# A fused attention, FFN and gated-convolution kernel: a new table of planner ranks and step durations, and eight instead of four ReLU buffers

## The chip, the cores and the metric

The kernel runs on one core of one Trainium2 chip. The metric is the device time of one execution in microseconds (us). The engines are named as in the profile: PE (TensorE matmul), PEld (its weight loads), DVE (VectorE), ACT (ScalarE), POOL (GpSimd) and SP (SyncE, which issues the DMAs here).

## What is computed

Three layers follow each other on 4 sequences of 576 positions with 512 features (18 tiles of 128 rows).

```python
q_rot, k_rot = rotate(q), rotate(k)               # 8 heads of 64
scores = (q_rot @ k_rot.T) / sqrt(64)
attn = exp(scores - max(scores)); attn /= attn.sum() + 1e-9
x = attn @ v                                      # heads side by side: 512 features
xn = (x - mean) / sqrt(var + 1e-6) * g_ln
x = x + relu(xn @ w_ch1) @ w_ch2                  # 512 -> 2048 -> 512, float64 weights
gate = sigmoid(causal depthwise convolution of x, 5 taps)
out = (gate * (x @ w_val)) @ w_out
```

## The kernel before, in words

**Attention.** The 576x576 score matrix of every head is cut into 144 tiles of 128 query rows. One tile passes through scores on PE (`a_scores`: L499 with float32 operands in batch 0, L504 with split float32r operands afterwards), the negated row maximum on DVE (`a_max`, L509), the exponential on ACT (`a_exp`, L515), its float16 part on ACT (`a_hi`, L521) and the rest of it on DVE (`a_lo`, L526), a transposing DMA issued by SP (`a_turn`, L531), and the product with V on PE (`a_pv`, L550 and L553). Before that q and k are rotated on DVE (`mul`, L314 and L316; `add`, L324; `lo`, L344), and V is scaled and split by ACT and DVE (L415, L441, L446, L450, L451); its scale comes from a maximum on DVE (`vmax0`, L424 and L137 to L139, for the four first ones together).

**Weights.** The FFN's float64 weights are loaded as 16 pieces of 1 MB (L649), put together by ACT and DVE (L658, L655, L662), bounded by matmuls on PE (`products`, L678, 128 of them), and split into two float16 halves (L716 on ACT, L719 on DVE).

**FFN.** For each of the 18 row tiles: LayerNorm on DVE, POOL and ACT (L786 to L809), a transposing DMA (L814), and then four times a step `f1` on PE (48 matmuls, L824), `relu` on ACT (L836, which writes `hh`), `hlo` on DVE (L842, which writes `hl`), and `f2` on PE (12 matmuls, L852). `ffn_out` on DVE adds the result (L856). `hh` and `hl` live in `FH` pairs of buffers; the four pairs of row tile 0 lie elsewhere.

**Gate and projection.** The last layer works on nine pairs of row tiles: a turn through `rope_sb` (DVE copy L948, DMA, DVE copy L960), two float32r halves (L968 on ACT, L973 on DVE), and then for four blocks of features the gate (ACT L979, four or eight taps on DVE in `gate_b`, L988, ACT sigmoid L992), the values (`val`, 12 matmuls on PE, L1001), their product (DVE L1006) and its halves (`val_b` ACT L1012, `val_c` DVE L1016, in one buffer `gv`), and at last `proj` on PE (L1028, twice 12 matmuls).

**What sets the order.** No hardware scheduler chooses. While the program is built, `plan.step` records every step with an engine, a duration that the author states, a rank and its dependencies; `Plan.run` replays them against those durations, and whenever an engine is free it takes, among the steps that are ready within `NEAR` us, the one of the lowest rank. SP's transfers have `RATE`, `T_LAG` and `AHEAD`. Ranks are a constant per kind of step (`R_SC`, `R_F1`, `R_GATE`, ...) plus a running number, and `..._LEAD` puts loads and rotations ahead of the tile that needs them. What comes out is one fixed list of instructions per engine, and every engine works through its own list in that order, waiting on semaphores. The constants stand at the head of the file.

Of the kernel before, what the change touches and what calls it, by code (L numbers as in the profile page):

```python
# [23 lines left out]
XN_SCALE = 2.0  # L24
W1_SCALE = 2.0 ** 10
W2_SCALE = 2.0 ** 15
PT, P16, FH = 4, 3, 4
QS, K_LEAD = 3, 6
T_LAG, RATE, NEAR, AHEAD = 2.4, 280.0, 0.15, 2.0
XT, KQ, RAW, GT, X3, GV = 3, 2, 3, 6, 2, 1  # L30

QK_LEAD_0, QK_LEAD, V_LEAD_0, V_LEAD, LD_LEAD, W_LEAD = 30, 8, 28, 6, 4, 6
R_W1, S_W1, R_W2, S_W2 = 3, 1, 16, 2
R_GAIN, R_TINY, R_LN, R_RELU, R_FO, R_OUT = 0, -900, -300, -200, -250, -20
R_SC, R_PV, R_F1, R_F2 = 0, -4, 1000, 900
# [17 lines left out]
class Plan:  # L53
# [3 lines left out]
    RATE, NEAR, AHEAD = RATE, NEAR, AHEAD  # L57
# [98 lines left out]
def kernel(ctx: ExitStack, tc: tile.TileContext, qk, v, g_ln, w_ch1, w_ch2, w_val, conv_w, w_out, rope, eye, out):  # L156
# [20 lines left out]
    plan = Plan(dict(raw0=RAW, raw=RAW, qx=2, qs=QS, kf0=1, kf1=1, kf2=1, kf3=1, qf=QS, k20=1, k21=1, k22=1, k23=1, kx0=1, kx1=1, kx2=1, kx3=1, kq=KQ, qd=1, qdf=1, vt0=NP, sv0=1, vt=1, vh=NP, sv=4, vb=2, vm=2, ss=2, so=1, nmx=4, p32=2, p16=P16, pT=PT,  # L177
                     hp=2, acc=1, wr0=3, wr1=2, ln=1, xn=1, x16=1, xT=XT, fh=FH, r3=4, t3=4, xT3=2, tx=1, x3=X3, gt=GT, gv=GV, pv=3, po=2))
# [3 lines left out]
    DVE, ACT, PE, SP, POOL = "DVE", "ACT", "PE", "SP", "POOL"  # L182
# [353 lines left out]
    def a_pv(i):  # L536
        p, h, c0 = tiles[i]
        pT = live.pop(i)
        vh, vl = prep_v(p)["vh"], prep_v(p)["vl"]
        g, j = group_of[i]  # L540
        if j == 0:
            ovs[g] = ps_o.tile([128, 6, D + 1], F32, name="ov", tag="ov")
        ov = ovs[g]
        if h is None:
            o, hs, nh = ov[:, 0:2], 0, 2
        else:
            j += tiles[groups[g][0]][1] is None
            o, hs, nh = ov[:, j:j + 1], h, 1
        for c in range(9):
            nc.tensor.matmul(o, pT[:, c], vh[:, 2 * c + hs:2 * c + hs + nh], start=(c == 0), stop=(c == 8))  # L550

            if c < 5:
                nc.tensor.matmul(o[..., 0:D], pT[:, c], vl[:, 2 * c + hs:2 * c + hs + nh], start=False, stop=False)  # L553
# [42 lines left out]
    for i in range(NS):  # L596
        p, h, c0 = tiles[i]
        b = parts[p][0]
        bf, vf = bufs[p], bufs[base[p]]
        if h != 1:  # L600
            ne = 1 if h is None else 2
            ss = [Buf("ss") for _ in range(ne)]
            x = plan.step(PE, (1.6 if h is None else 2.2) if b == 0 else 0.9 if h is None else 1.05, R_SC + i, lambda i=i: a_scores(i), after=bf["ready"] + ([bf["dg"]] if h is None else []), takes=ss,
                          uses=([bf["qd"]] if h is None else []) + [vf["kq"], bf["q"]], row="sc")
            attention.append(x)
            if p < NP:
                early.append(x)
            if b == 1:
                kx_users.append(x)
            for e in range(ne):  # L610
                j = i + e
                nm, p32, p16, pT = Buf("nmx"), Buf("p32"), Buf("p16"), Buf("pT")
                y = plan.step(DVE, dve(S), R_MX + j, lambda j=j: a_max(j), after=[x], takes=[nm], uses=[ss[e]])
                y = plan.step(ACT, act(S), R_EXP + j, lambda j=j: a_exp(j), after=[y], takes=[p32], uses=[nm, ss[e]], row="exp")
                y = plan.step(ACT, act(S), R_EXP + j, lambda j=j: a_hi(j), after=[y], takes=[p16], uses=[p32])
                y = plan.step(DVE, dve(S), R_LO + j, lambda j=j: a_lo(j), after=[y], uses=[p32, p16])
                y = plan.step(SP, 1.0, R_TURN + j, lambda j=j: a_turn(j), after=[y], takes=[pT], uses=[p16], size=TURN, row="turn")
                tile_done[j] = (y, pT)
    for g, ts in enumerate(groups):
        so = Buf("so")  # L620
        p = tiles[ts[0]][0]
        vf = bufs[base[p]]
        last = None
        for k, i in enumerate(ts):
            y, pT = tile_done[i]
            last = plan.step(PE, 0.82 if tiles[i][1] is None else 0.42, R_PV + i, lambda i=i: a_pv(i), after=[y, last] + vf["v"], takes=[so] if k == 0 else [], uses=[pT, vf["vh"]] + ([so] if k else []), row="pv")
        b, pr, n, lead, m = out_of(g)
        x = plan.step(DVE, 0.24 + m * 0.14 + (0.1 if m else 0), R_OUT + ts[-1], lambda g=g: a_rd(g), after=[last], uses=[so, vf["sv"]])
        o = [x]
        if lead:  # L630
            o.append(plan.step(ACT, 0.32, R_OUT + ts[-1], lambda g=g: a_lead(g), after=[x], uses=[so]))
        outs[g] = o
        attention.extend(o)
# [235 lines left out]
    for n in range(NT):  # L869
        ln, xn, x16, xT, acc = Buf("ln"), Buf("xn"), Buf("x16"), Buf("xT"), Buf("acc")  # L870
        x = plan.step(DVE, 1.0, R_LN + n, lambda n=n: ln_a(n), after=rows[n] + [e_ffn], takes=[ln], row="ln")
        x = plan.step(POOL, 1.3, R_LN + n, lambda n=n: ln_p(n), after=[x], uses=[ln])
        x = plan.step(DVE, 0.47, R_LN + n, lambda n=n: ln_b(n), after=[x], takes=[xn], uses=[ln])
        x = plan.step(ACT, act(512), R_LN + n, lambda n=n: ln_c(n), after=[x], takes=[x16], uses=[xn])
        x = plan.step(DVE, dve(512), R_LN + n, lambda n=n: ln_d(n), after=[x], uses=[xn, x16])
        x = plan.step(SP, 1.0, R_LN + n - 100, lambda n=n: ln_t(n), after=[x], takes=[xT], uses=[x16], size=TURN)
        f2s = None
        prev = None
        for f in range(0, KF, FE):
            k = n * 4 + f // FE  # L880
            hp, fh = Buf("hp"), Buf("fh")
            prev = plan.step(PE, 2.7, R_F1 + k, lambda n=n, f=f: f1(n, f), after=[x, w_ready[0, f // 2 + 1], prev], takes=[hp] + ([fh] if n else []), uses=[xT], row="f1")
            y = plan.step(ACT, act(512), R_RELU + k, lambda n=n, f=f: relu(n, f), after=[prev], uses=[hp] + ([fh] if n else []), row="relu")
            y = plan.step(DVE, dve(512), R_RELU + k, lambda n=n, f=f: hlo(n, f), after=[y], uses=[hp] + ([fh] if n else []))
            f2s = plan.step(PE, 2.6, R_F2 + k, lambda n=n, f=f: f2(n, f), after=[y, w_ready[1, f // 2 + 1], f2s], takes=[acc] if f == 0 else [], uses=([acc] if f else []) + ([fh] if n else []), row="f2")
            if n == 0:
                pend_hid[5 + f // FE] = f2s
        done.append(plan.step(DVE, dve(512), R_FO + n, lambda n=n: ffn_out(n), after=[f2s], uses=[acc]))
# [245 lines left out]
```

## Time and profile before

| what | value |
|---|---|
| time, median of 3 runs | 742.03 us (741.21 to 745.29) |
| profiled execution | 743.6 us, of which the span from first to last instruction is 741.8 us |
| mean granted TensorE clock | 0.961 of full speed |
| busy PE, PEld, DVE, ACT, POOL | 681.0, 531.2, 631.1, 459.3, 16.9 us |
| DMA | 103.62 MB, 66.3% of 16 engines over the span |

A busy time is the time in which the engine had an instruction in work, and the ends of matmuls are modelled, so a PE that is shown busy may hold a matmul that waits. "Granted clock" is the share of the full TensorE clock. A window row gives busy time and number of instructions for every engine in one stretch of the span.

### The profile page before, as it was taken

The numbers are of one execution on the slowest core, as the hardware profiler recorded it, in microseconds if no ns is written. First come the engines' busy times: TensorE is split into PE (matmuls) and PEld (weight loads), VectorE is DVE, ScalarE is ACT, GpSimd is POOL, SyncE is SP. The second block draws the span as 40 slices with busy tenths as digits, with TensorE's granted clock in tenths as the row PEclk, the third lists the DMA queues.
The fourth block names the chain that finished last, engine by engine and source line by source line (L and its number), as shares of the span: only waits on it lengthen the run. The fifth ranks groups of instructions, "written<-read, shape, count | busy, mean of one in ns | idle before, by whom it ended". The sixth has DMA issues, their size and how long they took to land.

```text
span 741.8 us, 19303 instructions
## 1 busy us (share of the span) xinstructions
PE 681.0 (92%) x7929; PEld 531.2 (72%) x7929; DVE 631.1 (85%) x1365; ACT 459.3 (62%) x802; POOL 16.9 (2%) x40
## 2 busy tenths in 40 slices
PE   3446879899999999999999999999999989999998
PEld 1334768557777787778777877787777867787886
DVE  6999989999898999989998988987566999877664
ACT  5888976869666577757567876665282443344332
POOL 0000000000000000000000000000000000000000
PEclk9965878999999999999999999999999998999999
DMA  8999997578887997779869778865574132221011
GB/s 307 259 296 271 281 218 158 93 179 132 153 133 139 163 163 150 132 133 166 156 133 193 140 109 134 137 111 97 110 206 73 29 86 58 58 57 44 30 43 57
DMA packets 239288, 103.62 MB, mean 140 GB/s; under 512 B 211168, under 2 KB 227552, under 8 KB 239200
## 3 DMA queue, kind: packets, MB, share of 16 engines
q1 hardware_dynamic: 239200, 102.39, 66.3%
q8 instruction: 62, 1.02, 0.6%
q14 instruction: 26, 0.21, 0.1%
HBM read 45.73 MB, written 4.72 MB: 68 GB/s over the span
## 4 chain that ended last, share of the span: by engine, by line
PE 56%; DVE 28%; ACT 7%; DMA 5%; issue 3%; SPq 0%; ACTq 0%; DVEq 0%
PE hp L824 16%; PE acc L852 16%; PE po L1028 6%; PE sc L504 5%; DVE gt L988 4%; PE pv L1001 4%; PE ov L550 4%; DVE p L526 4%; DVE nmx L509 3%; DMA pT<-p 3%; DVE raw L316 2%; PE ov L553 2%; ACT p L521 2%; ACT p L515 2%; DVE hl L842 2%
## 5 line engine op out<-in xcount | busy, mean ns | idle before, releaser
L824 PE MATMUL hp<-xT,wall 128*128 128x128 f16 x3456 | 206.3, 220 | 0.0
L824 PEld LDWEIGHTS <-wall 128*128 128x128 f16 x3456 | 196.8, 98 | 6.7 <-issue 2.0
L852 PE MATMUL acc<-wall,hh 128*128 128x512 f16 x544 | 163.8, 383 | 2.1 <-DVE gt L988 2.1
L515 ACT ACTIVATE p<-sc,nmx 128x576 f32<-128x576 f32 x144 | 105.8, 736 | 68.0 <-DVE nmx L509 66.8
L526 DVE SCALAR_TENSOR_TENSOR p<-p,p 128x576 f16<-128x576 f32 x144 | 108.1, 753 | 21.4 <-ACT p L521 21.0
L509 DVE TENSOR_REDUCE nmx<-sc 128x1 f32<-128x576 f32 x144 | 106.1, 749 | 1.6 <-PE sc L504 0.9
L852 PE MATMUL acc<-wall,hl 128*128 128x512 f16 x272 | 104.1, 383 | 1.5 <-DVE hl L842 1.5
L550 PE MATMUL ov<-vh,pT 128*128 128x65 f16 (+1 forms) x1296 | 94.8, 201 | 10.9 <-DMA pT<-p 6.2
L521 ACT ACTIVATE p<-p 128x576 f16<-128x576 f32 x144 | 97.8, 682 | 5.0 <-DMA pT<-p 1.9
L550 PEld LDWEIGHTS <-pT 128*128 128x128 f16 x1296 | 80.4, 100 | 25.3 <-issue 10.6
L852 PEld LDWEIGHTS <-hh 128*128 128x128 f16 x544 | 49.0, 98 | 51.8 <-ACT hh L836 2.3
L988 DVE SCALAR_TENSOR_TENSOR gt<-xT,cw,gt 128x256 f32<-128x256 f32 (+4 forms) x192 | 72.3, 412 | 6.8 <-ACT gt L979 4.3
L553 PE MATMUL ov<-vl,pT 128*128 128x64 f16 (+1 forms) x720 | 69.5, 201 | 0.0
L836 ACT ACTIVATE hh<-hp 128x512 f16<-128x512 f32 x68 | 40.0, 588 | 32.7 <-PE hp L824 32.5
L553 PEld LDWEIGHTS <-pT 128*128 128x128 f16 x720 | 53.9, 101 | 4.1 <-issue 0.4
L842 DVE SCALAR_TENSOR_TENSOR hl<-hp,hh 128x512 f16<-128x512 f32 x68 | 46.6, 685 | 8.6 <-ACT hh L836 8.5
L852 PEld LDWEIGHTS <-hl 128*128 128x128 f16 x272 | 26.8, 98 | 36.5 <-DVE hl L842 4.6
L992 ACT ACTIVATE gt<-gt 128x256 f32<-128x256 f32 x36 | 15.0, 417 | 54.9 <-DVE gt L988 54.9
L1028 PE MATMUL po<-woh,gv 128*128 128x512 f32 x144 | 48.3, 406 | 0.0
L316 DVE TENSOR_TENSOR raw<-raw,rope_sb 128x256 f32<-128x256 f32 (+2 forms) x64 | 43.1, 673 | 0.3 <-DMA raw<-in_qk_dram 0.3
L1001 PE MATMUL pv<-xh,wvh 128*128 128x256 f32 x144 | 42.2, 293 | 0.0
L1001 PE MATMUL pv<-xl,wvh 128*128 128x256 f32 x144 | 40.4, 281 | 0.0
(131 smaller groups left out, 981.6 us busy)
## 6 DMA issues: line engine op xcount, KB each, us to landing
raw<-in_qk_dram SPq DMA_DIRECT2D x16, 576.0 KB, 4.4
raw<-in_qk_dram SPq DMA_DIRECT2D x48, 128.0 KB, 2.8
wall<-in_moe_w_ch_dram SPq DMA_DIRECT2D x6, 1024.0 KB, 7.7
xw<-in_moe_w_ch_dram SPq DMA_DIRECT2D x6, 1024.0 KB, 7.1
vt<-in_v_dram SPq DMA_DIRECT2D x16, 320.0 KB, 3.8
out_dram<-x SPq DMA_DIRECT2D x18, 256.0 KB, 2.0
kk<-in_moe_w_ch_dram SPq DMA_DIRECT2D x4, 1024.0 KB, 5.9
raw<-in_qk_dram SPq DMA_DIRECT2D x16, 192.0 KB, 3.5
```

Source lines behind the costliest of these rows:

```text
L509: nc.vector.tensor_reduce(out=nmx, in_=sc[:, :, 0:HS], axis=AX.XY, op=ALU.max, negate=True)
L515: nc.scalar.activation(out=p32.rearrange("p (e n) -> p e n", e=2), in_=sc[:, :, 0:HS], func=ACTF.Exp, bias=nmx)
L521: nc.scalar.activation(out=p16[:, 0], in_=p32, func=ACTF.Copy, scale=P_SCALE)
L526: nc.vector.scalar_tensor_tensor(out=p16[:, 1], in0=p32, scalar=P_SCALE, in1=p16[:, 0], op0=ALU.mult, op1=ALU.subtract)
L550: nc.tensor.matmul(o, pT[:, c], vh[:, 2 * c + hs:2 * c + hs + nh], start=(c == 0), stop=(c == 8))
L553: nc.tensor.matmul(o[..., 0:D], pT[:, c], vl[:, 2 * c + hs:2 * c + hs + nh], start=False, stop=False)
L824: nc.tensor.matmul(hp[:, j], w1[:, u, wl * 512 + o:wl * 512 + o + 128], xT[:, xl * KD + c], start=(i == 0), stop=(i == 3 * KD - 1))
L842: nc.vector.scalar_tensor_tensor(out=hl, in0=hp, scalar=0.0, in1=hh, op0=ALU.max, op1=ALU.subtract)
L852: nc.tensor.matmul(st["acc"], lw[:, j], w2[:, f + j, lo * 512:lo * 512 + 512], start=(f + j == 0 and i == 0), stop=(f + j == KF - 1 and i ...
L988: nc.vector.scalar_tensor_tensor(out=gt[:, c0:c1], in0=xT[:, c, HALO + c0 - s:HALO + c1 - s], scalar=col(KT - 1 - s, c), in1=gt[:, c0:c1], ...
L1001: nc.tensor.matmul(pv, lw[:, d, c * 128:(c + 1) * 128], rx[:, d], start=(n == 0), stop=(n == 3 * KD - 1))
L1028: nc.tensor.matmul(po, lw[:, d, sl], rx[:, d, :], start=(n == 0), stop=(n == 3 * KD - 1))
```

## The change

Two things are edited. `FH`, the number of buffer pairs for the outputs of the ReLU, goes from 4 to 8. And the numbers that steer `Plan.run` are replaced: nearly every rank and lead, the tolerance `NEAR`, `AHEAD`, and the stated durations of four kinds of PE steps (scores, P.V and f2). No instruction is added or removed: both programs hold the same steps with the same shapes, 3456 matmuls at L824, 864 at L852, 144 maxima, and so on.

```diff
-PT, P16, FH = 4, 3, 4
-QS, K_LEAD = 3, 6
-T_LAG, RATE, NEAR, AHEAD = 2.4, 280.0, 0.15, 2.0
+PT, P16, FH = 4, 3, 8
+QS, K_LEAD = 3, 1.48
+T_LAG, RATE, NEAR, AHEAD = 2.4, 280.0, 0.02, 2.54
...
-R_SC, R_PV, R_F1, R_F2 = 0, -4, 1000, 900
+R_SC, R_PV, R_F1, R_F2 = 0, -14.98, 3025.09, 448.32
...
-R_TW, R_X3, R_GATE, R_VAL, R_VALD, R_PROJ = 0, 100, 200, 800, 50, 800
+R_TW, R_X3, R_GATE, R_VAL, R_VALD, R_PROJ = -113.05, 104.96, -267.39, 1701.75, -190.59, 664.42
...
-            x = plan.step(PE, (1.6 if h is None else 2.2) if b == 0 else 0.9 if h is None else 1.05, R_SC + i, lambda i=i: a_scores(i), after=bf["ready"] + ([bf["dg"]] if h is None else []), takes=ss,
+            x = plan.step(PE, (1.2 if h is None else 2.2 if i < 24 else 1.5) if b == 0 else 0.9 if h is None else 1.06, R_SC + i, lambda i=i: a_scores(i), after=bf["ready"] + ([bf["dg"]] if h is None else []), takes=ss,
...
-            last = plan.step(PE, 0.82 if tiles[i][1] is None else 0.42, R_PV + i, lambda i=i: a_pv(i), after=[y, last] + vf["v"], takes=[so] if k == 0 else [], uses=[pT, vf["vh"]] + ([so] if k else []), row="pv")
+            last = plan.step(PE, 0.87 if tiles[i][1] is None else 0.47, R_PV + i, lambda i=i: a_pv(i), after=[y, last] + vf["v"], takes=[so] if k == 0 else [], uses=[pT, vf["vh"]] + ([so] if k else []), row="pv")
```

What this does to the lists shows at two places. The first is DVE's list near the start of the program, from the second rotated k (`kf`) on, where the first two score tiles get their maxima. Before:

```order
L324 TENSOR_TENSOR kf<-raw 128x576
L509 TENSOR_REDUCE nmx<-sc 128x1 x2
L314 SCALAR_TENSOR_TENSOR raw<-raw,rope_sb 128x2x128
L324 TENSOR_TENSOR qx<-raw 128x128
L424 TENSOR_REDUCE vm_196<-va_189 128x4
L137 TENSOR_SCALAR vs_m<-vm_196 128x4
L138 RECIPROCAL vs_m<-vs_m 128x4
L139 TENSOR_SCALAR sv_198<-vs_m 128x4
L316 TENSOR_TENSOR raw<-raw,rope_sb 128x1152
L446 SCALAR_TENSOR_TENSOR vl<-vt,sv_198,vh 128x640 x2
```

After:

```order
L324 TENSOR_TENSOR kf<-raw 128x576
L509 TENSOR_REDUCE nmx<-sc 128x1 x2
L526 SCALAR_TENSOR_TENSOR p_183<-p_176,p_183 128x576
L424 TENSOR_REDUCE vm_200<-va_195 128x4
L137 TENSOR_SCALAR vs_m<-vm_200 128x4
L138 RECIPROCAL vs_m<-vs_m 128x4
L139 TENSOR_SCALAR sv_202<-vs_m 128x4
L526 SCALAR_TENSOR_TENSOR p_191<-p_185,p_191 128x576
L314 SCALAR_TENSOR_TENSOR raw<-raw,rope_sb 128x2x128
L446 SCALAR_TENSOR_TENSOR vl<-vt,sv_202,vh 128x640
```

The `a_lo` of the first tile (L526) moved right behind its maximum, ahead of the next q's rotation (L314 and L324 qx) and of V's scale.

The second place is DVE's list around the first gate of the last layer (L988 on the first `xT` tile), where the end of the FFN (L842, L856) and the turn of the rows (L948, L960) meet. Before:

```order
L948 COPY rope_sb<-x_67 128x1024 x2
L842 SCALAR_TENSOR_TENSOR hl<-hp,hh 128x512
L960 COPY xT_10117<-tx 128x2x4x128
L948 COPY rope_sb<-x_67 128x1024
L842 SCALAR_TENSOR_TENSOR hl<-hp,hh 128x512
L856 SCALAR_TENSOR_TENSOR x_4630<-acc,scl,x_4630 128x512
L960 COPY xT_10117<-tx 128x2x4x128
L948 COPY rope_sb<-x_67 128x1024
L973 TENSOR_TENSOR xl_10191<-xT_10117,xh_10190 128x1024
L842 SCALAR_TENSOR_TENSOR hl<-hp,hh 128x512
L988 SCALAR_TENSOR_TENSOR gt<-xT_10117,cw,gt 128x255
```

After:

```order
L948 COPY rope_sb<-x_67 128x1024 x2
L809 SCALAR_TENSOR_TENSOR x_9849<-xn,x_9849 128x512
L842 SCALAR_TENSOR_TENSOR hl<-hp,hh 128x512
L856 SCALAR_TENSOR_TENSOR x_4437<-acc,scl,x_4437 128x512
L960 COPY xT_9919<-tx 128x2x4x128
L948 COPY rope_sb<-x_67 128x1024
L842 SCALAR_TENSOR_TENSOR hl<-hp,hh 128x512
L960 COPY xT_9919<-tx 128x2x4x128
L948 COPY rope_sb<-x_67 128x1024
L988 SCALAR_TENSOR_TENSOR gt<-xT_9919,cw,gt 128x255
```

The taps of the gate moved ahead of the halves of the values (L973), and the whole block moved forward against the FFN: fourteen `hl` (L842) follow the first tap in the new list, ten in the old one.

## Rows read from the trace of the kernel before

**Rows 1.** Busy time by stage: start, head, middle, end of FFN, first gates, rest.
```profile
0.00:20.00 20.00, 6.82 (x24) 3.55 (x24) 12.93 (x22) 10.97 (x20) 1.02 (x10) 1.00 0.89 313
20.00:181.60 161.60, 123.89 (x1385) 94.22 (x1385) 152.27 (x304) 130.49 (x197) 3.80 (x8) 0.84 0.93 211
181.60:429.20 247.60, 244.72 (x3337) 189.52 (x3336) 226.16 (x498) 169.38 (x303) 8.25 (x18) 1.00 0.80 148
429.20:569.10 139.90, 139.90 (x1887) 108.14 (x1886) 104.19 (x218) 78.55 (x138) 3.86 (x5) 1.00 0.68 125
569.10:614.50 45.40, 42.63 (x367) 33.18 (x365) 43.95 (x107) 21.41 (x44) 0.00 (x0) 0.95 0.28 59
614.50:741.80 127.30, 123.09 (x941) 102.58 (x938) 91.64 (x222) 48.53 (x104) 0.00 (x0) 0.99 0.18 51
```

**Rows 2.** Chain of waits: start us, us, piece; score groups that bound the middle, and one f1.
```profile
181.63 1.00 PE sc L504 x12
...
189.56 2.70 PE hp L824 x48
...
429.21 0.99 PE sc L504 x12
```

**Rows 3.** Timeline of DVE and ACT near the start of the program.
```profile
12.12 1.42 DVE L509 TENSOR_REDUCE nmx<-sc 128x1 f32<-128x576 f32 x2 [0.32 <-PE sc L499]
...
14.76 0.69 DVE L424 TENSOR_REDUCE vm<-va 128x4 f32<-128x512 f32 x1 [0.55 <-PE va L420]
...
12.91 0.74 ACT L515 ACTIVATE p<-sc,nmx 128x576 f32<-128x576 f32 x1 [0.99 <-DVE nmx L509]
13.55 0.73 ACT L415 ACTIVATE vh<-vt 128x640 bf16<-128x640 f32 x1
14.18 0.19 ACT L415 ACTIVATION_READ_ACCUMULATOR vh<-vt 128x1 f32 x1
14.27 0.67 ACT L521 ACTIVATE p<-p 128x576 f16<-128x576 f32 x1
14.84 0.73 ACT L515 ACTIVATE p<-sc,nmx 128x576 f32<-128x576 f32 x1
```

**Rows 4.** Groups of DVE instructions by line and shape: count, busy us, mean ns.
```profile
L509 DVE TENSOR_REDUCE nmx<-sc 128x1 f32<-128x576 f32 x144 | 106.1, 749 | 1.6 <-PE sc L504 0.9 <-PE sc L499 0.3
L526 DVE SCALAR_TENSOR_TENSOR p<-p,p 128x576 f16<-128x576 f32 x144 | 108.1, 753 | 21.4 <-ACT p L521 21.0
L316 DVE TENSOR_TENSOR raw<-raw,rope_sb 128x1152 f32<-128x1152 f32 x16 | 21.6, 1349 | 0.3 <-DMA raw<-in_qk_dram 0.3
L344 DVE SCALAR_TENSOR_TENSOR k<-raw,k 128x576 fp32r<-128x576 f32 x8 | 6.0, 749 | 0.0
L856 DVE SCALAR_TENSOR_TENSOR x<-acc,scl,x 128x512 f32<-128x512 f32 x18 | 13.4, 746 | 2.9 <-PE acc L852 2.8
L842 DVE SCALAR_TENSOR_TENSOR hl<-hp,hh 128x512 f16<-128x512 f32 x68 | 46.6, 685 | 8.6 <-ACT hh L836 8.5
L988 DVE SCALAR_TENSOR_TENSOR gt<-xT,cw,gt 128x256 f32<-128x256 f32 x80 | 38.6, 483 | 4.9 <-ACT gt L979 2.8
```

**Rows 5.** Windows of 20 us: low clock; the two fullest of DVE during attention.
```profile
40.00:60.00 20.00, 10.61 (x84) 7.45 (x85) 18.20 (x42) 17.83 (x23) 0.00 (x0) 0.59 1.11 324
60.00:80.00 20.00, 12.92 (x145) 11.08 (x145) 19.17 (x45) 15.80 (x22) 0.93 (x1) 0.56 1.06 274
120.00:140.00 20.00, 19.84 (x222) 13.65 (x220) 19.69 (x35) 13.57 (x20) 0.73 (x2) 1.00 0.62 113
260.00:280.00 20.00, 20.00 (x296) 16.01 (x295) 19.39 (x44) 13.20 (x23) 1.31 (x3) 1.00 0.99 155
```

**Rows 6.** Chain of waits in the last layer: f2, projection and value steps on PE.
```profile
611.80 4.45 PE acc L852 x10
616.25 5.95 PE po L1028 x24
...
633.38 2.61 PE acc L852 x12
635.99 5.60 PE po L1028 x24
...
716.98 8.55 PE pv L1001 x72
```

More of the change, by code (lines that the diff above doesn't have):

```diff
@@ L26 @@
 W2_SCALE = 2.0 ** 15
-PT, P16, FH = 4, 3, 4
-QS, K_LEAD = 3, 6
-T_LAG, RATE, NEAR, AHEAD = 2.4, 280.0, 0.15, 2.0
+PT, P16, FH = 4, 3, 8
+QS, K_LEAD = 3, 1.48
+T_LAG, RATE, NEAR, AHEAD = 2.4, 280.0, 0.02, 2.54
 XT, KQ, RAW, GT, X3, GV = 3, 2, 3, 6, 2, 1
-QK_LEAD_0, QK_LEAD, V_LEAD_0, V_LEAD, LD_LEAD, W_LEAD = 30, 8, 28, 6, 4, 6
-R_W1, S_W1, R_W2, S_W2 = 3, 1, 16, 2
-R_GAIN, R_TINY, R_LN, R_RELU, R_FO, R_OUT = 0, -900, -300, -200, -250, -20
-R_SC, R_PV, R_F1, R_F2 = 0, -4, 1000, 900
-R_MX, R_EXP, R_LO, R_TURN = 0, -1, -2, -20
-R_TW, R_X3, R_GATE, R_VAL, R_VALD, R_PROJ = 0, 100, 200, 800, 50, 800
+QK_LEAD_0, QK_LEAD, V_LEAD_0, V_LEAD, LD_LEAD, W_LEAD = 181.27, 3.17, -6.32, -4.39, 12.06, 6.51
+R_W1, S_W1, R_W2, S_W2 = 8.31, 0.16, 9.07, 3.13
+R_GAIN, R_TINY, R_LN, R_RELU, R_FO, R_OUT = 20.06, -900, -555.11, -708.58, -681.24, -47.51
+R_SC, R_PV, R_F1, R_F2 = 0, -14.98, 3025.09, 448.32
+R_MX, R_EXP, R_LO, R_TURN = -9.34, -9.08, -4.81, -5.45
+R_TW, R_X3, R_GATE, R_VAL, R_VALD, R_PROJ = -113.05, 104.96, -267.39, 1701.75, -190.59, 664.42
 class Buf:
@@ L884 @@
             y = plan.step(DVE, dve(512), R_RELU + k, lambda n=n, f=f: hlo(n, f), after=[y], uses=[hp] + ([fh] if n else []))
-            f2s = plan.step(PE, 2.6, R_F2 + k, lambda n=n, f=f: f2(n, f), after=[y, w_ready[1, f // 2 + 1], f2s], takes=[acc] if f == 0 else [], uses=([acc] if f else []) + ([fh] if n else []), row="f2")
+            f2s = plan.step(PE, 2.62, R_F2 + k, lambda n=n, f=f: f2(n, f), after=[y, w_ready[1, f // 2 + 1], f2s], takes=[acc] if f == 0 else [], uses=([acc] if f else []) + ([fh] if n else []), row="f2")
             if n == 0:
```

## The prediction, made before the changed kernel was run

> **What bounds the kernel now.** I read the windows by stage first, then the chain of waits, then DVE's own rows. The stages [rows 1] have different limits. In the head (20 to 181.6 us) DVE is busy 152.27 of 161.6 us, 94.2%, PE only 123.89; PE waits for what DVE has not yet made (rotated q and k, maxima, weight halves). In the middle (181.6 to 429.2) PE is busy 244.72 of 247.6 us and DVE 226.16, 91.3%. From there to 569.1, when the attention runs out, PE is never idle and DVE idles 35.7 us of 139.9. Then come the first gates: DVE is busy 43.95 of 45.4 us and PE falls short. In the rest PE is busy 123.09 of 127.3 us, and the last few us lie behind the last matmul. So PE sets the time wherever it is full, and the time above PE's own work is lost in the head and at the first gates. A change of order can win only there, and it can lose wherever it makes PE wait in a stage that is now full.
>
> **How I cost a change of order.** Neither program has an instruction that the other lacks, so busy sums stay. What moves is how much DVE work stands ahead of a given PE step. I counted, in both lists, the PE steps done and the DVE instructions that must be done by the same point (through the semaphores, over ACT and the DMAs). The sum is made against the profiled execution, 743.6 us, which is 1.6 above the median of the three runs, 742.03; the forecast is for the median. About 0.5% (3.7 us) is what a measurement of this kernel can tell from no change.
>
> **1. Start of the program: +2.2 us.** In the old list the first two maxima (at 12.12 us, 1.42 us long) [rows 3] are followed by a q rotation, which covers most of ACT's exponential and copy. In the new list a_lo (L526) follows at once. ACT gives its input at 14.27 + 0.67 = 14.9 us, so DVE stands from about 13.5 to 14.9, 1.4 us. Then the maximum over V (L424) needs the fourth V sum, which in the new ACT list stands behind the second exponential: that ends at 15.6, the sum's 0.73 + 0.19 run to 16.5, and with the 0.39 us that lay between the sum's end (14.37) and L424 (14.76) before, L424 starts at 16.9; DVE stands 1.3 us more. Before, the two waits shown there were 0.55 and 0.32, the second of which stays. 1.4 + 1.3 - 0.55 = 2.2 us later, nothing behind it hides it because DVE is the bound in the head. Bounds: 0 (if a later DMA wait, hidden before by DVE's work, swallows it) and 2.7.
>
> **2. Head: -4.6 us.** The score group at 181.63 us [rows 2] is a point at which both lists hold the same PE work: 10 f1, 8 f2, 37 P.V tiles, all 128 weight-bound matmuls and the same score matmuls. Ahead of it the new list has one large rotation (1.35 us), one `lo` of k twice over (2 x 0.75), one FFN sum (0.75) and four smaller rotation instructions (0.55, 0.75, 0.35 and 0.35 by their width against these rows) fewer, and one `hl` (0.69) more [rows 4]: 4.9 us by row means. Rows of DVE overlap a little: two maxima take 1.42 us [rows 3] where two means make 1.50. Seven instructions less 0.08 each leaves 4.3 us, and at the head's 94.2% that is 4.6 us of time. Bounds: -4.9, and 0 if the loads set the pace, since the DMA engines' share is 0.93 in this stage [rows 1]. I take the DVE figure: PE's waits there end with DVE instructions in the chain, and the loads ahead of this point are fewer in the new list too (26.8 MB against 28.0, with 40 transposes in both).
>
> Ahead of this the eight buffers matter: in the old list at most four ReLU outputs wait for their f2 (besides row tile 0), in the new one six, so more f1 stand in front of the point at which the second weight matrix is ready. That is part of the 4.6, not a term of its own.
>
> **3. Clock: 0.** PE had its clock at 0.59 and 0.56 of full on average from 40 to 80 us, after it had been busy only 10.61 and 12.92 of 20 us [rows 5]; full and half are 2.4 and 1.2 GHz. The new list puts PE's early work in almost the same places. Bounds are +-2.6 us, the idle time of DVE in those 40 us (40 - 18.20 - 19.17), as PE's speed counts only where DVE waits for it. I take 0. The Trainium skill (TensorE: Matmul & The Clock Gate, "What's actually happening") says the throttled state is the default and activity releases it; by that rule PE work packed earlier would have its clock earlier, and the sum would be up to 2.6 us lower.
>
> **4. Middle: 0, and this is the open term.** The next comparable point is the score group at 429.21 us [rows 2]. At equal PE work (within 1 us) the new list is there six P.V tiles and three score groups ahead, two f1 and one f2 behind. That takes six maxima and six a_lo more on DVE (12 x 0.75, less the overlap: 8.1 us) [rows 4], and one LayerNorm, one preparation of V and two output divisions, less one `hl`, which at `hl`'s 0.69 for a whole-tile instruction and 0.2 for a small one is about 4 us: 12.1. It came 4.3 behind, so it must do 16.4 us more in the same PE time: 226.16 + 16.4 = 242.6 us of DVE work in 247.6. The two fullest windows of DVE during attention are 19.69 and 19.39 of 20 us [rows 5], 98.5% and 97%. At these the stage takes 246.3 or 250.1 us, -1.3 or +2.5. I take 98%, no change. Bounds: -2.9 (PE's own idle there) and +9.9 (94.2%, the head's rate: 257.5 us).
>
> **5. First gates: -4.5 us.** From 569.1 to 614.5 us PE loses 2.77 us idle, an f2 of which 10 matmuls are recorded over 4.45 us where 10 of 12 of a free one take 2.2, and a projection of 5.95 instead of 5.60 [rows 1, 6]: 5.4 us together. Where PE's list has finished 60 f1, 59 f2 and all attention, the new list has the first 16 taps, 7.7 us [rows 4], and some smaller steps already behind it. They moved into the stage before, where DVE idles 35.7 us [rows 1]. And fourteen `hl` instead of ten follow the first tap, so f1 and f2 lie between the value steps and give DVE time. The stage then asks 43.95 - 7.7 = 36.3 us of DVE, less than the 40.0 that PE needs. Bounds -5.4 and 0; I take most of it.
>
> **6. End: +1 us.** At the end the new list has projection, six value steps, projection, four value steps, projection, one value step, projection. The halves of the product go through the one `gv` buffer, which a projection frees, and the next projection waits behind eight taps (8 x 0.48 = 3.9 us) as well. Before, 72 value matmuls ran 8.55 us without a wait [rows 6]. Bounds 0 and 3.9; I take 1.
>
> **Sum.** 2.2 - 4.6 + 0 + 0 - 4.5 + 1 = -5.9 us; 743.6 - 5.9 = 737.7, less 1.6 is **736 us**.
>
> **Rivals.** *DVE becomes the bound of the middle (slower).* One mechanism: 16.4 us more DVE work in a stage where PE had no room. For it: DVE takes its list in order, so an a_lo that waits for ACT (21.0 us in total before [rows 4]) holds back every `hl` behind it, and PE then lacks its f2. Against it: two windows at 97% and more. It decides once DVE stays under 95.9% there (242.6/0.959 = 253 us, the whole gain) and makes the kernel slower by over 0.5% under 94.5%. At the head's 94.2% the time is 736 + 9.9 = 746 us. The Trainium skill speaks for this rival: Perfetto Trace Analysis, "Identifying the Most-Contended Engine", holds matmul busy time for a poor measure of PE and wants its weight loads (here 189.52 of 247.6 us, 77% [rows 1]) beside VectorE's occupancy (91.3%). By that rule DVE is already the most contended engine of the middle, and the change loads it further. Against the rule, an f1 still takes 2.70 us there [rows 2] with nothing between its 48 matmuls, so PE has no 23% in hand. Chance 0.17.
>
> *The wait at the first gates only moves (741 us).* In the new list DVE has almost 13 us of work between two `hl` of that stage, about what PE has between them; if an f2 then waits where a projection waited, term 5 is 0: 736 + 4.5 = 741. Chance 0.18.
>
> *Everything fits (730 us).* The late start is swallowed, the middle loses PE's 2.9 us of idle, the gates give all 5.4: 743.6 - 4.6 - 2.9 - 5.4 + 1 - 1.6 = 730. For it: DVE's waits in the middle are mostly its own waits for ACT, which a tighter list can fill. Chance 0.20.
>
> *The eight buffers do nothing.* The count of six outputs in flight speaks against it; its price is 0 and it changes no term.
>
> **How the numbers follow.** My case has the remaining 0.45. The range is 728 to 746 us: the low end holds the case in which everything fits and 2 us for the clock, the high end DVE at the head's rate in the middle; what lies outside is that rate together with a full 3.9 at the end, or term 2 at 0. Below 738.3 lie 0.8 of my case and the case that fits (0.56) and a little of the others: faster 0.57. Above 745.7 lies most of the DVE rival: slower 0.15. The rest, 0.28, is the same.
>
> **What would show it.** Right: DVE reaches the score group with 10 f1 and 8 f2 behind it at about 179 us; DVE is busy 97 to 98% between that and the later score group; the stretch with the first gates has no projection that waits for a tap; f2 near 611 us takes 2.6 us. Wrong: PE idle growing beyond 5 us between 180 and 430 with DVE as the releaser, a first gate stage with 3 us or more of PE idle, or waits of several us at the last three projections.

## The result and the profile after

| | before | after |
|---|---|---|
| median of 4 runs each, on one chip | 742.56 us (741.21 to 745.29) | 735.18 us (734.00 to 736.51) |
| profiled execution (span) | 743.6 us (741.8) | 735.05 us (733.3) |
| busy PE, DVE, ACT | 681.0, 631.1, 459.3 us | 674.5, 624.4, 454.6 us |

The ratio of after to before is 0.9897, 95% interval 0.9863 to 0.993: the change makes the kernel 1% faster. The forecast was 736 us. The time came out as forecast, its parts did not: the head gains more, the middle costs something, and the end gains where a loss was priced.

**One measure for all lists.** Both programs do the same PE work in another order, so the same clock time is not the same place. I aligned every recorded matmul with its place in PE's list and added up, ahead of each step, the PE work at full clock (spacing of matmul starts in the trace of before: an f1 2.68 us, an f2 2.59, 28 P.V matmuls 0.88, 12 score matmuls 0.995, a value step 1.44, a projection 5.71, which is 24 times the usual 0.238, and so on, the same prices for every run). The start of a step less this sum is the **loss** of PE up to there. Where two traces have the same PE work behind them, the difference of losses is the time won or lost. A loss can be slightly negative: a projection of the changed kernel takes 5.60 us. The span of the pair above went from 741.8 to 733.3, 8.5 us, and the loss says where:

| stretch | loss before | loss after | change | predicted |
|---|---|---|---|---|
| start and head, up to the score group with 10 f1 and 8 f2 behind it | 86.2 | 79.4 | -6.7 | 2.2 - 4.6 = -2.4 |
| from there to 330 us of PE work | 6.6 | 8.5 | +1.9 | 0 |
| on to the last P.V step | 0.7 | 3.2 | +2.6 | nothing priced |
| last P.V step to 530 us of PE work (first gates) | 5.8 | 0.6 | -5.1 | -4.5 |
| from there to the last projection's start | 0.3 | -0.8 | -1.1 | +1 |

**Stages.** These are the windows of the changed kernel by stage (start and length; busy time and count of PE, PEld, DVE, ACT, POOL; granted clock, DMA share, GB/s), against [rows 1]. The borders 174.8 and 424.3 have the PE work behind them that 181.6 and 429.2 had; 515.3 is the last P.V step, 560.4 the first value step:

```profile
0.00:20.00 20.00, 3.79 (x16) 2.00 (x16) 11.04 (x21) 9.13 (x17) 1.01 (x10) 1.00 0.87 288
20.00:174.80 154.80, 123.20 (x1391) 92.65 (x1391) 147.77 (x297) 128.89 (x194) 3.07 (x8) 0.89 0.93 220
...
174.80:424.30 249.50, 244.80 (x3357) 190.43 (x3357) 235.97 (x525) 177.17 (x326) 9.48 (x18) 1.00 0.85 156
424.30:515.30 91.00, 89.07 (x1250) 68.73 (x1248) 68.57 (x154) 48.91 (x83) 3.00 (x4) 1.00 0.65 111
515.30:560.40 45.10, 45.10 (x544) 33.89 (x542) 33.41 (x62) 25.51 (x47) 0.55 (x1) 1.00 0.54 135
560.40:606.00 45.60, 44.92 (x396) 35.92 (x395) 41.45 (x100) 17.03 (x36) 0.00 (x0) 1.00 0.29 60
```

Up to the score group DVE was busy 12.93 + 152.27 = 165.20 us before [rows 1] and stood 16.4; now 158.81 and 16.0. So DVE is busy 6.4 us less ahead of that point, and stands as long as before.

Not all of that is less work. A busy time counts the overlap of two rows once. In the changed kernel two maxima in a row overlap by 0.08 us (median) in all 35 places, while L569 starts 0.03 us behind the end of L568, whose result it reads, in all 64. Over the whole run the durations of DVE's 1365 rows add up to 701.2 us before and 700.4 after, but its busy time to 631.1 and 624.4: 857 pairs of neighbours overlapped before, 933 do now. Overlap alone makes no faster kernel: `e2` and `e12` below have 925 and 928 such pairs and are slower than before.

The group's row in the timeline of PE (start, length, in brackets the idle time and its releaser where there is one), which answers to the first row of [rows 2]:

```profile
174.78 1.14 PE L504 MATMUL sc<-kx,qs 64*128 64x288 f32 x12
```

**Start.** DVE's timeline of the changed kernel, against [rows 3]:

```profile
12.04 1.42 DVE L509 TENSOR_REDUCE nmx<-sc 128x1 f32<-128x576 f32 x2 [0.32 <-PE sc L499]
14.89 0.76 DVE L526 SCALAR_TENSOR_TENSOR p<-p,p 128x576 f16<-128x576 f32 x1 [1.43 <-ACT p L521]
16.59 0.69 DVE L424 TENSOR_REDUCE vm<-va 128x4 f32<-128x512 f32 x1 [0.94 <-PE va L420]
```

The stall of 1.43 us and the late maximum over V (16.59 for 14.76) are there as forecast, and DVE is busy 1.9 us less in the first 20 us. But it stands 7.0 us instead of 9.3 between there and the score group: the late start is swallowed.

**Middle.** DVE's share is now 235.97 of 249.5 us, 94.6%, for 91.3% before. DVE waits less for ACT than in [rows 4]:

```profile
L526 DVE SCALAR_TENSOR_TENSOR p<-p,p 128x576 f16<-128x576 f32 x144 | 106.6, 751 | 14.5 <-ACT p L521 13.7
L509 DVE TENSOR_REDUCE nmx<-sc 128x1 f32<-128x576 f32 x144 | 104.8, 748 | 4.2 <-PE sc L504 3.2 <-PE sc L499 0.8
```

PE waits more. Its waits from the score group to the last P.V step (line and what it waited for; total us, times, longest):

```profile
PE ov L550 <- DMA pT<-p: 2.2, 4, 0.8
PE hp L432 <- ACT vh L415: 2.1, 4, 0.8
PE ov L550 <- DVE x L573: 1.6, 2, 1.4
```

Before, the same stretch (181.6 to 533.4 us) had 1.3 us for `pT` and 0.7 for L432 and nothing for L573. With the small ones PE's listed waits grew from 2.7 to 6.7 us, about as much as the loss. The three shown are attention steps that wait for their own chain; f2 waits 0.2 us in all. The longest, at 467.0 us, in the two timelines: the division of an output (L568 to L573) stands on DVE behind an `a_lo` and an FFN sum, and the P.V step behind it needs its buffer.

```profile
464.79 0.75 DVE L526 SCALAR_TENSOR_TENSOR p<-p,p 128x576 f16<-128x576 f32 x1
465.46 0.74 DVE L856 SCALAR_TENSOR_TENSOR x<-acc,scl,x 128x512 f32<-128x512 f32 x1
466.12 0.21 DVE L568 TENSOR_SCALAR rd<-ov,sv 128x2 f32<-128x2 f32 x1
466.36 0.17 DVE L569 RECIPROCAL rd<-rd 128x2 f32<-128x2 f32 x1
466.56 0.29 DVE L573 TENSOR_TENSOR x<-ov,rd 128x128 f32<-128x128 f32 x1
```

```profile
467.00 0.19 PE L550 MATMUL ov<-vh,pT 128*128 128x65 f16 x1 [1.39 <-DVE x L573]
```

**Last layer.** PE's waits from 556 us to the end are one row:

```profile
PE acc L852 <- DVE hl L842: 0.7, 2, 0.4
```

Before there were 2.1 us behind a tap and 1.2 behind `hl` from 569 us on. The timeline of PE and a window (columns as in [rows 1]) of the kernel before at that tap:

```profile
610.13 1.03 PE L852 MATMUL acc<-wall,hh 128*128 128x512 f16 x2 [2.14 <-DVE gt L988]
```

```profile
610.50:617.00 6.50, 5.87 (x15) 2.40 (x14) 6.50 (x19) 2.51 (x5) 0.00 (x0) 0.51 0.20 39
```

Behind the wait the granted clock was 0.51, nearly the lower of its two levels, 1.2 GHz. The f2 matmuls stand 0.43 us apart there for 0.216 elsewhere, so of the 5.8 us lost before some 2 (ten matmuls, an estimate) are a slower PE and not a wait. In the changed kernel neither is left; its clock is 1.00 in all the stages above from 174.8 to 606 us.

In the chain of waits the f2, projection and value rows that answer to [rows 6] have no hole of a microsecond left; a pattern of f2, value, f2, value, projection, value, f1, value, f1 repeats from 595 to 697 us:

```profile
578.34 2.33 PE acc L852 x10
580.67 1.43 PE pv L1001 x12
582.10 5.59 PE po L1028 x24
...
595.98 2.59 PE acc L852 x12
598.57 1.43 PE pv L1001 x12
...
697.30 8.45 PE pv L1001 x72
```

### The profile page after: what moved, and what is told of

Same layout as the page of the kernel before. It is cut to its first block, busy times and chain, and to the rows that moved or that the text cites. A ratio compares the mean times of both kernels' runs of the same rounds, so it can differ in the third digit from the quotient of the medians.

```text
span 733.3 us, 19313 instructions
## 1 busy us (share of the span) xinstructions
PE 674.5 (92%) x7929; PEld 527.4 (72%) x7929; DVE 624.4 (85%) x1365; ACT 454.6 (62%) x802; POOL 17.1 (2%) x40
## 4 chain that ended last, share of the span: by engine, by line
PE 44%; DVE 36%; ACT 7%; DMA 7%; issue 5%; SPq 1%; DVEq 0%; ACTq 0%
PE hp L824 12%; PE acc L852 11%; PE po L1028 7%; DVE p L526 7%; DVE nmx L509 6%; PE pv L1001 6%; DMA pT<-p 4%; DVE raw L316 3%; PE sc L504 2%; DVE hl L842 2%; PE ov L550 2%; DVE gt L988 2%; ACT p L515 2%; DMA raw<-in_qk_dram 2%; DVE wall L719 2%
## 5 line engine op out<-in xcount | busy, mean ns | idle before, releaser
L824 PE MATMUL hp<-xT,wall 128*128 128x128 f16 x3456 | 206.7, 220 | 0.0
L824 PEld LDWEIGHTS <-wall 128*128 128x128 f16 x3456 | 196.7, 98 | 5.8 <-issue 2.3
L852 PE MATMUL acc<-wall,hh 128*128 128x512 f16 x544 | 161.9, 379 | 0.2 <-DVE x L856 0.2
L526 DVE SCALAR_TENSOR_TENSOR p<-p,p 128x576 f16<-128x576 f32 x144 | 106.6, 751 | 14.5 <-ACT p L521 13.7
L852 PE MATMUL acc<-wall,hl 128*128 128x512 f16 x272 | 103.1, 379 | 0.7 <-DVE hl L842 0.7
L550 PE MATMUL ov<-vh,pT 128*128 128x65 f16 (+1 forms) x1296 | 93.1, 199 | 9.9 <-DMA pT<-p 7.2
L521 ACT ACTIVATE p<-p 128x576 f16<-128x576 f32 x144 | 95.7, 679 | 6.5 <-DMA pT<-p 4.7
L550 PEld LDWEIGHTS <-pT 128*128 128x128 f16 x1296 | 79.3, 100 | 25.8 <-issue 10.4
L852 PEld LDWEIGHTS <-hh 128*128 128x128 f16 x544 | 48.9, 98 | 49.6 <-issue 1.2
L988 DVE SCALAR_TENSOR_TENSOR gt<-xT,cw,gt 128x256 f32<-128x256 f32 (+4 forms) x192 | 72.0, 413 | 6.7 <-ACT gt L979 4.1
L553 PEld LDWEIGHTS <-pT 128*128 128x128 f16 x720 | 53.1, 100 | 4.5
L842 DVE SCALAR_TENSOR_TENSOR hl<-hp,hh 128x512 f16<-128x512 f32 x68 | 46.5, 684 | 9.5 <-ACT hh L836 9.2
L852 PEld LDWEIGHTS <-hl 128*128 128x128 f16 x272 | 26.6, 98 | 33.9 <-DVE hl L842 2.1
L1001 PE MATMUL pv<-xh,wvh 128*128 128x256 f32 x144 | 43.5, 302 | 0.0
L1001 PE MATMUL pv<-xh,wvl 128*128 128x256 f32 x144 | 40.4, 280 | 0.0
```

The source lines that it names most:

```text
L521: nc.scalar.activation(out=p16[:, 0], in_=p32, func=ACTF.Copy, scale=P_SCALE)
L526: nc.vector.scalar_tensor_tensor(out=p16[:, 1], in0=p32, scalar=P_SCALE, in1=p16[:, 0], op0=ALU.mult, op1=ALU.subtract)
L824: nc.tensor.matmul(hp[:, j], w1[:, u, wl * 512 + o:wl * 512 + o + 128], xT[:, xl * KD + c], start=(i == 0), stop=(i == 3 * KD - 1))
L988: nc.vector.scalar_tensor_tensor(out=gt[:, c0:c1], in0=xT[:, c, HALO + c0 - s:HALO + c1 - s], scalar=col(KT - 1 - s, c), in1=gt[:, c0:c1], ...
L1001: nc.tensor.matmul(pv, lw[:, d, c * 128:(c + 1) * 128], rx[:, d], start=(n == 0), stop=(n == 3 * KD - 1))
```

## The experiments

The theory after the result: the ranks move DVE work out of the head, the middle pays part of it back by its own order, and the tail's ranks remove the wait at the first gates. The rivals: the middle pays because of the head's debt; the buffers carry the head's gain; or the tail gains only by what the middle leaves it.

**Parts of the change by themselves.** `e1`:

```diff
-PT, P16, FH = 4, 3, 4
+PT, P16, FH = 4, 3, 8
```

> The kernel before with eight buffers for ReLU outputs and nothing else changed; its list comes out instruction for instruction as before on PE and DVE, so only waits for a free buffer can go. Theory (the buffers matter only through the order that the planner makes with them): same time as before within 0.3%, 742 +- 2 us. Rival (in the old list the four buffers hold ACT back between 127 and 148 us, where the kernel before lost 6 us against PE's own work that the changed one did not lose): 2 to 6 us faster, 736 to 740.

742.65 us, ratio 1.0002 (0.9987 to 1.0016). Nothing: with the old list the four buffers hold nobody back.

`e2` puts four buffers into the changed kernel (`FH` 8 to 4).

> The changed kernel with four buffers again, all ranks and durations kept; its list is the same up to some 75 PE steps (about 130 us) and differs from there, since the planner may not have more than four outputs in flight. Theory (six outputs in flight let PE run f1 while the second weight matrix is not ready, which is where the head gains between 127 and 148 us): the head loses 3 to 6 us of its gain, 738 to 741 us. Rival (the gain of the head comes from the ranks, which put less DVE work ahead): 735 +- 1.5 us.

751.51 us, ratio 1.0109 (1.0084 to 1.0134). Both theory and rival missed: four buffers cost 16 us against the change, and make it slower than before. By the loss, the head gives back 3 to 4 us, the middle is 5 worse than in the change, and the tail loses 8.3 where the change loses nothing. With the limit the planner makes another list from PE's 1066th matmul of 7929 on. That the ranks suit that list less is a guess: what in it costs the middle 5 us was not followed.

`e3` puts the last layer's ranks back:

```diff
-R_TW, R_X3, R_GATE, R_VAL, R_VALD, R_PROJ = -113.05, 104.96, -267.39, 1701.75, -190.59, 664.42
+R_TW, R_X3, R_GATE, R_VAL, R_VALD, R_PROJ = 0, 100, 200, 800, 50, 800
```

> The changed kernel with the six ranks of the last layer as before; the list is the same up to PE step 370 of 434 (about 540 us). Theory (the first gates are paid for by the tail's own ranks, which put taps before the point where they are waited for): the stretch with the first gates loses 4 to 5 us again, 739 to 740 us. Rival (the tail gains because DVE has less left to do when the attention runs out): 735 to 736 us.

739.47 us, ratio 0.9959 (0.9945 to 0.9973), and the loss is at the first gates, 3.7 us: the theory's number. The chain of waits of this run there; the f2 waits 2.0 us for the FFN sum (L856), which frees the accumulator and stands behind taps. Then it takes 4.23 us for 2.59: the granted clock was 0.57 from 577 to 581 us. So 2.0 of the 3.7 us are the wait and 1.6 the clock behind it:

```profile
573.65 0.48 DVE gt L988
574.13 0.60 DVE hl L842
574.74 0.65 DVE xT L960
575.38 0.64 DVE x L856
...
576.06 4.23 PE acc L852 x12
580.30 5.79 PE po L1028 x24
```

`e4` brings the relations between those ranks into the kernel before:

```diff
-R_TW, R_X3, R_GATE, R_VAL, R_VALD, R_PROJ = 0, 100, 200, 800, 50, 800
+R_TW, R_X3, R_GATE, R_VAL, R_VALD, R_PROJ = -113, 105, -150, 985, -120, 975
```

> The kernel before with the ranks of the last layer put into the same relations as in the change (second FFN product before projection before value before first FFN product on PE; gates first, then value outputs, then weight halves on DVE); the list is that of before up to PE step 373 of 426 (about 545 us). Theory (the tail's ranks alone are worth the term of the first gates): PE loses nothing there, 737 to 738 us, unless the value steps left at the end, four in a row between projections, are held by taps; then 739 to 743. Rival (they do nothing without the rest): 742 us.

745.12 us, ratio 1.0034 (1.0023 to 1.0045). That is above all that was expected. The gates still lose 4.0 us and the steps after the last f2 3.7. The tail's ranks don't do it alone.

**Stages by themselves.** For `e5` to `e11` every rank, lead, tolerance and stated duration of the changed kernel that differs from before is a pair, and the planner changes over at counts of planned P.V steps (37 is the score group, 144 the last step; the table below says who plans what). All seven have eight buffers. The core of the diff against the changed kernel, for `e8`:

```diff
-R_SC, R_PV, R_F1, R_F2 = 0, -14.98, 3025.09, 448.32
+R_SC, R_PV, R_F1, R_F2 = 0, Two(-14.98, -4), Two(3025.09, 1000), Two(448.32, 900)
...
-                x = min((x for r, x in can if r <= t + self.NEAR), key=lambda x: (x.rank, x.order))
+                x = min((x for r, x in can if r <= t + now(self.NEAR)), key=lambda x: (now(x.rank), x.order))
...
             done.append(x)
+            pv += "a_pv" in x.fn.__code__.co_freevars
+            Two.NOW = int(37 <= pv < 144)
```

> One list made of two sets of ranks: those of the change (with their stated durations) until 37 P.V steps are planned, the point of the score group on which the prediction's terms 2 and 4 rest, and those of before from there on; eight buffers. PE's list is that of the change for 109 steps. Theory (the head's gain is real and stays, the middle of the change loses because of its own order): 742.7 less 5 to 6.5 = 736 to 738 us. Rival (the head gains by putting off work that DVE must then do in the middle, whatever the ranks there): the gain is 6 us at 175 us and 0 to 2 us at the end, 741 to 743.

738.99 us, ratio 0.9949 (0.993 to 0.9967), between the two. The middle on old ranks loses 8.1 us behind the new head, for 7.0 behind the old one, so there is next to no debt. The tail, on old ranks, loses 6.0.

> Ranks of before up to 37 P.V steps, those of the change from there to the last of the 144 P.V steps, those of before after it. Theory (the middle loses by its own order): 742.7 + 2 to 4 = 745 to 747 us. Rival (it loses only because the new head puts work off): 741 to 743, since DVE has no debt here.

765.15 us, ratio 1.0293 (1.0274 to 1.0313): far outside both. The middle loses 17.7 us and the tail, on old ranks, 18.1; its longest wait there is one of 6.5 us for the first half of the values (L1034 behind ACT's L1001). PE's waits in the middle of this run (the lines stand 33 further down in `e5` to `e11`: L583 is P.V, L606 the division):

```profile
PE ov L583 <- DVE x L606: 4.2, 5, 1.7
PE ov L583 <- DMA pT<-p: 2.4, 3, 1.0
```

> Ranks of before up to the last of the 144 P.V steps, all ranks of the change after it, so that the relations of the last layer's ranks to those of the FFN are the change's. Theory (the order of the tail alone removes the loss at the first gates): 742.7 - 5 = 737 to 739 us. Rival (the gates need DVE to have done more before the attention ends, as the run with the new relations alone, which lost 4 us there, says): 741 to 744.

744.13 us, ratio 1.0016 (1.0005 to 1.0028): the rival's figure. PE loses 3.2 us at the first gates and 1.5 later.

> Ranks of the change in the head and the tail, those of before from 37 to 144 P.V steps. Theory (terms add up, the middle's own order costs 2 to 4 us): 735.2 - 2 to 4 = 731 to 733 us, better than both. Rival (the pieces only fit together: the middle of the change leaves DVE ahead for the gates and takes up the head's debt): 736 to 741.

743.16 us, ratio 1.0009 (0.9995 to 1.0022): 2 us beyond the rival's range even, and the place is plain. This run has the lowest loss of all at the last P.V step, 89.0 us, and loses 9.2 behind it. From 660 us on PE waits for the product (L1039) and the half (L1049) of values whose taps are late:

```profile
PE pv L1034 <- DVE gt L1039: 3.5, 2, 2.8
PE po L1061 <- DVE gv L1049: 1.8, 3, 0.7
```

In this list only 16 f1 and 16 f2 are left when the attention ends, 21 in the change, 18 before. The f1 and f2 that stand between value steps give DVE time for the taps; here they run out, and 23 of the 36 value steps stand after the last f2, where the change has 12. So I took the number of products left as the new theory and varied it, with the new ranks in the tail.

> Ranks of the change, with those of before only from 60 to 144 P.V steps. After the last P.V step this list has 18 f1 and 18 f2 left, and 17 value steps stand after the last f2 (the change: 21 and 12; the run with all of the middle on old ranks: 16 and 23, and there PE lost 9 us in the tail against 0 in the change). Theory (what the middle of the change pays for is FFN products left over, which cover DVE's taps in the last layer): half of that loss, 3 to 6 us in the tail, 737 to 740 us. Rival (the tail's loss has to do with the middle's state, not with how many products are left): 742 to 744, as with 16.

> Ranks of the change, with those of before only from 90 to 144 P.V steps: 20 f1 and 21 f2 are left after the last P.V step, 15 value steps stand after the last f2. Theory (products left cover the taps): 1 to 3 us lost in the tail, 735 to 738 us. Rival (as above): 742 to 744.

> Ranks of the change, with those of before only from 120 to 144 P.V steps, the stretch in which the middle of the change lost 2.4 us where before lost 0.7: 21 and 21 products are left, 12 value steps after the last f2, as in the change. Theory: no loss in the tail and up to 2 us less before it, 733 to 735.5 us, the version that may beat both. Rival (the old ranks lose in the tail): 740 or more.

> The change with the stated durations of before for score, P.V and second FFN steps; all else kept. The list differs from PE step 43 on; 22 and 22 products are left, 8 value steps after the last f2. Theory (ranks were chosen together with these durations, so another list comes out that was not chosen; attention is taken further ahead, as the one more product left shows): the middle loses 2 to 8 us more and the tail nothing, 737 to 743 us. Rival (the durations do nothing by themselves): 735 +- 1.5 us.

They gave 738.95 (0.9942, 0.9923 to 0.9962), 738.85 (0.9941, 0.9926 to 0.9956), 735.31 (0.9891, 0.9873 to 0.991) and 748.34 us (1.0075, 1.0057 to 1.0093). `e9` and `e11` are as the theory said, `e10` is 0.9 us above it, `e12` far above. `e12` undoes the stated durations of the score, P.V and f2 steps. All by the loss, in us (the middle is from the score group to the last P.V step, for `e2` and `e12` from 94 us of PE work on, the tail from there to the last projection's start, in `e7` to `e10` to that of the last two, which stand side by side and lose another 1 us; "list" says by letter whose numbers plan the head, the middle and the tail, n for new):

| run | list | f2 left | value steps after last f2 | loss at score group | middle | tail | median |
|---|---|---|---|---|---|---|---|
| before | o o o | 18 | 7 | 86.2 | 7.3 | 6.0 | 742.56 |
| e1 | o o o | 18 | 7 | 86.3 | 6.9 | 5.0 | 742.65 |
| e4 | o o mixed | 18 | 17 | 85.6 | 6.8 | 8.0 | 745.12 |
| e7 | o o n | 18 | 17 | 86.0 | 7.1 | 4.7 | 744.13 |
| e6 | o n o | 24 | 4 | 85.4 | 17.7 | 18.1 | 765.15 |
| e5 | n o o | 16 | 11 | 82.3 | 8.1 | 6.0 | 738.99 |
| e8 | n o n | 16 | 23 | 80.7 | 8.3 | 9.2 | 743.16 |
| e9 | n, o from 60, n | 18 | 17 | 81.3 | 8.0 | 6.3 | 738.95 |
| e10 | n, o from 90, n | 21 | 15 | 82.3 | 11.4 | 1.6 | 738.85 |
| e11 | n, o from 120, n | 21 | 12 | 80.7 | 10.8 | -0.2 | 735.31 |
| after | n n n | 21 | 12 | 79.4 | 11.7 | -0.2 | 735.18 |
| e3 | n n mixed | 21 | 12 | 80.5 | 12.9 | 3.5 | 739.47 |
| e12 | n n n, old durations | 22 | 8 | 83.4 | 11.9 | 7.8 | 748.34 |
| e2 | n n n, 4 buffers | 22 | 8 | 83.8 | 16.9 | 8.3 | 751.51 |

With the new ranks in the tail, 16, 18, 21 products left lose 9.2, 4.7 to 6.3, and -0.2 to 1.6 us there, as the theory of cover says. More is not better: `e12`, with 22 left, loses 7.8 us in the tail, where I expected nothing, and no more than the change in the middle, where I expected 2 to 8; and `e6`, with 24 left and the old tail, loses most of all. So the count goes with the loss in six lists and is not shown to be its cause. The longest waits of PE in `e12` from 540 us on, and the place on DVE and PE:

```profile
PE acc L852 <- DVE x L856: 3.1, 3, 2.0
PE pv L1001 <- DVE xl L973: 1.3, 2, 1.0
```

```profile
577.12 0.68 DVE L842 SCALAR_TENSOR_TENSOR hl<-hp,hh 128x512 f16<-128x512 f32 x1
577.72 2.17 DVE L988 SCALAR_TENSOR_TENSOR gt<-xT,cw,gt 128x64 f32<-128x64 f32 x8
579.81 0.75 DVE L856 SCALAR_TENSOR_TENSOR x<-acc,scl,x 128x512 f32<-128x512 f32 x1
```

```profile
580.61 0.59 PE L852 MATMUL acc<-wall,hh 128*128 128x512 f16 x2 [2.03 <-DVE x L856]
```

Eight short taps stand ahead of the FFN sum, and the first f2 of the next row tile waits 2.03 us for the accumulator. The same hole of 2.0 to 2.1 us before that f2 is in `e2`, `e3`, `e7` and `e9`. A row tile takes four f2, and `e2`, `e7`, `e9` and `e12` have 18 or 22 left, so that a row tile ends at the same place among the first gates; the change, `e10` and `e11`, with 21, have no such hole, but `e3`, with 21, has it. That the count modulo four decides is therefore not shown. What the traces show is that an FFN sum behind taps at the first gates makes the next f2 wait some 2 us, in these five lists; in three of them (`e2`, `e3`, `e9`) the clock fell behind the wait, to 0.57 to 0.66 over 4 to 5 us. Why `e12` and `e2` lose another 3 to 4 us before the last projections was not followed further.

No run is faster than the change: `e11` saves 1 us in the middle at most, and its median is the same.

## Why the prediction was right, and where its steps failed

That the time came out at 735.2 for 736 is in good part luck, since the terms' errors mostly cancel. In the profiled pair start and head gain 4.3 us more than priced and the end 2.1, and the middle costs 4.5 that were priced at 0. The gates alone came near their price.

**1, the start (+2.2), failed in its effect.** The stall came as computed, 1.43 us for 1.4, L424 at 16.59 for 16.9. What failed is "nothing behind it hides it because DVE is the bound in the head". DVE was busy only 94.2% there, and its later waits took the delay up; the lower bound of 0 was right.

**2, the head (-4.6), had the right sign and size, and its working was off.** DVE is busy 6.4 us less ahead of the score group, not 4.3. The instructions were counted almost rightly: one small sum more (L324, 0.35 us) is missing from DVE's list there, 5.3 us by row means for 4.9. What failed is "busy sums stay", and the 0.08 us that I took off for every row: the new order makes more rows overlap, so overlap adds to the saving instead of lessening it. The lists with the new head stand at 79.4 to 82.3, mean 81.0, those with the old one at 85.4 to 86.3, mean 85.9. So -6.7 of the pair is partly one execution's luck; over 12 executions start and head are worth -4.9, twice the predicted -2.4 and close to term 2 alone.

**3, the clock (0), was right where I looked and not further on.** The granted clock of the head rose from 0.84 to 0.89. Most of it lies where [rows 5] had 0.59 and 0.56, and where PE is now busier (10.61 and 12.92 us there before):

```profile
40.00:60.00 20.00, 12.79 (x111) 8.63 (x110) 19.10 (x46) 15.35 (x23) 0.99 (x1) 0.66 1.13 300
60.00:80.00 20.00, 14.66 (x191) 12.17 (x192) 19.41 (x40) 18.20 (x24) 0.00 (x0) 0.82 0.93 229
```

The Trainium skill (TensorE: Matmul & The Clock Gate, "What's actually happening") has activity release the clock, and these rows agree. The rows of `e7` below do not bear it out: PE is hardly busier there than before, and at full clock. In this stretch the clock was worth nothing. `e7` has before's list of PE up to the score group, ran at full clock there, and stands at the group at a loss of 86.0 us for 86.2:

```profile
40.00:60.00 20.00, 11.73 (x102) 8.53 (x99) 18.26 (x42) 17.75 (x23) 0.00 (x0) 1.00 1.11 325
60.00:80.00 20.00, 12.91 (x147) 10.89 (x147) 19.26 (x45) 16.11 (x22) 0.99 (x1) 1.00 0.96 281
```

Later in the head it did count. The kernel before had a granted clock of 0.57 from 142 to 146 us, behind a wait of PE of 1.67 us for V's preparation (L432 behind L415): four score matmuls took 2.29 us for 1.19 in the changed kernel, an f1 3.38 for 2.85, 1.6 us together. All five executions with the old head have a mean clock of 0.97 from 125 to 180.8 us, all seven with the new one 1.00 from 125 to 174.8. So up to 1.6 of the 4.9 us, an estimate, are the clock, which comes back as that wait goes; no run separates it from term 2.

**4, the middle (0), was mis-sized, and it did not end where I let it end.** Two lists with all the new ranks give 11.7 and 12.9, four lists with the old ones 6.8 to 7.3: +5, inside the bounds of -2.9 and +9.9. Half of the pair's 4.5 lies behind 429 us in before, where I priced nothing because PE was never idle there. The work was counted well: the instructions that moved make 14.8 us by before's row means, for 16.4. But DVE's busy time rose by 9.8 only (235.97 for 226.16), because 377 pairs of its rows overlap there and 314 did. It ran at 94.6%, near the head's rate that the first rival took and not at 98%. That rival had the direction; its price of 9.9 was too high, because DVE's busy time grew less than its work. Its mechanism is shown in part. The division above is held up in DVE's order, and in `e6` P.V steps wait five times for one (4.2 us). But the f2 that lacks its `hl` behind a waiting `a_lo` did not come: f2 waits 0.2 us, and DVE's waits for ACT at L526 fell from 21.0 to 13.7 us. The Trainium skill (Perfetto Trace Analysis, "Identifying the Most-Contended Engine") calls matmul busy time a poor measure and goes by occupancy for VectorE. By that rule, the trace agrees in sign alone: DVE's share went from 91.3 to 94.6%, and PE lost some 5 of 345 us more.

**5, the first gates (-4.5), held:** -5.1, with the projection at 5.59 us and f2 with no hole. But the reason was half. Of the 5.4 us that I took for waits, some 2 were the clock behind a wait, and they went with it; `e7`, with a wait of 2.1 us and full clock, loses 3.2 there. And I put the term to the tail's own order. `e4` and `e7` have that order and lose 3 to 4 us all the same; `e3` has the new head and middle without it and loses 3.7. It takes both. In the window of the first gates DVE was busy 41.45 of 45.6 us, not 36.3.

**6, the end (+1), failed:** -1.1. The `gv` buffer, which I took for the next wait, holds nothing up: 72 value matmuls run 8.45 us, as before.

**The buffers.** "The eight buffers do nothing", price 0, holds for the old list (`e1`) and is wrong for the new one, by 16 us (`e2`). Six outputs in flight was the right thing to have counted, and I drew no price from it.

## What to carry to other kernels

The terms of a list's change do not add: new ranks for the head alone were worth 3.6 us, for the middle alone they cost 22 to 23, for the tail alone they cost 1.5, and all together they gain 7. Before a stage is tuned by itself, count what it leaves to the next one (here FFN products among the taps, though their number alone did not decide), and price a stage's loss together with the later stage that lives on it. Compare two orders at equal work of the engine that bounds, not at equal times, and take several executions before 2 us of one stage are believed. A busy time is not a sum of work: where order changes, compare the rows' durations and their overlaps as well.

## What the runs showed that I had not expected

A buffer limit that costs nothing with one list costs 16 us with another. The same 1365 DVE instructions can be busy 7 us less by their order alone. A clock of 0.59 and 0.56 over 40 us cost nothing where DVE is the bound, and one of 0.57 over 4 us elsewhere some 1.6 (an estimate). And one execution says little of one stage: the seven lists that are alike up to the score group stand there at losses from 79.4 to 82.3 us, and the same list in the last layer (before and `e1`) lost 6.0 and 5.0; behind the same wait its clock was 0.51 and 0.76 from 610 to 617 us.
